# Banks next to each other, loads without held transfers, and a new order of issue in a fused attention and channel-mix kernel

## The chip, the cores and the metric

The kernel runs on one core of one Trainium2 chip. The metric is the device time of one execution in microseconds (us), less is better. Three runs of the kernel before gave 128.08, 128.44 and 128.81 us. A further execution was taken with the hardware profiler; all rows below are from that one.

The core has five engines, each with a queue of its own that is worked off strictly in order: PE (matrix products, results to PSUM only), DVE (vector), ACT (scalar), POOL (GpSimd, which does not touch PSUM here) and SP (here it only issues transfers). They meet through semaphores. PSUM has eight banks of 512 float32 for each of 128 partitions.

## The reference

Two layers in a row, for 4 batches, 4 heads, 1088 positions and head size 32:

```python
def phi(x):                                  # sketch of degree 2: r = 8, so 64 features
    a = einsum('rd,bhsd->bhsr', S1, x)
    b = einsum('rd,bhsd->bhsr', S2, x)
    return einsum('bhsi,bhsj->bhsij', a, b).reshape(..., 64)
q_p, k_p = phi(q), phi(k)
kv  = einsum('bhsf,bhsd->bhfd', k_p, v)      # 64 x 32 for each head
num = einsum('bhsf,bhfd->bhsd', q_p, kv)
den = einsum('bhsf,bhf->bhs', q_p, k_p.sum(axis=2)) + 1e-6
x   = (num / den) as [4, 1088, 128]

xk = mu_k * x + (1 - mu_k) * x_prev          # x_prev: one position earlier
xr = mu_r * x + (1 - mu_r) * x_prev
k  = relu(xk @ w_k)                          # 128 -> 1024
v  = (k * k) @ w_v                           # 1024 -> 128
out = sigmoid(xr @ w_r) * v
```

## The kernel before, in words

Everything is one long list of small tasks, the string `ORDER` (L26). Each entry names a function, its indices, the engine that is to do it (`V` DVE, `A` ACT, `G` POOL, `P` DVE reading PSUM directly) and, after `@`, the PSUM banks that it writes. A loop at L583 calls the functions in that order. The order of the list is the order in which each engine gets its instructions; a tracker in the framework adds a semaphore wait wherever an instruction touches a tile that an instruction of another engine has written or still reads. All of PSUM is one tile, `PS`, of eight banks.

The first stage works batch by batch (0 to 3). For the keys: transposes `kt` on DVE, projection `kproj` on PE, copy `abev`, outer product `kp` (POOL or DVE), and `kvmm` on PE, then `kvev`, `kdmm`, `kdev` which lay `kv` out as weights in `kvw`. For the denominators: `zmm`, `zev`, `wmm`, `wsq`. For the queries: `qt`, `abw` on PE, copy `abwev`, then `pw`, `den`, `an` and the outer product `qp`. The result x is built by PE transposes `pt`, copies `ptev`, the product `xp` into a pair of banks, its copy `xpev`, and `tt`, `ttev`, `xt`, `xtev`, `xs` for the last 64 positions of each batch. Batch 3 takes another way: transposes `tr` on DVE and the product `xn` into four banks, copied by `xnev`.

The second stage works on 9 groups of columns: two groups of 512 for each batch, and group 8 of 256 with the last positions of all batches. `xk` and `xr` mix x with its shift (on POOL this is two instructions, L483 and L488; on DVE one, L491, L493 or L496). `f1.g.c` (L523) makes one of four parts of the hidden layer: two products of 128x512 into a pair of banks. `relu.g.c` (L529) on ACT turns both banks of the pair into a bf16 tile `k1` (six buffers). `sq.g.c` squares it into `k2` (eight buffers), on DVE at L264 or on ACT at L538. `f2.g.c` (L550) multiplies with `wv`, eight products of 128x128, and accumulates over c in one bank for each group. `rr` (L559) and `sig` (L565) make the gate, `fin` (L568) multiplies on DVE, `st` (L578) stores.

The pair of banks is a view of `PS` with a stride: `f1.2.1@24` writes banks 2 and 4 through `PS[:, 2:5:2]`, and `relu.2.1` reads both in one instruction:

```python
    def pair(banks, n):
        i, j = banks
        return PS[:, i:j + 1:j - i, :n]
```

Before the first stage, `zz` (L191) multiplies zeros into a bank that nobody reads. The loads are issued by SP in the order of `LOADS` (L24). An entry with a `+` is a transfer of four bytes out of a tile that is being loaded into `held` (L159): SP can issue it, and so all that stands behind it, only when that load has landed.

## Time and profile before

| | |
|---|---|
| median of three runs (lowest, highest) | 128.44 us (128.08, 128.81) |
| the profiled execution | 127.39 us |
| its span, first to last instruction | 125.6 us |
| mean granted PE clock in the span | 0.903 |
| busy PE, DVE, ACT, POOL | 88.4, 76.1, 61.5, 50.0 us |
| first product of the second stage (`f1.0.1`) starts | 29.83 us |
| last `relu` starts | 120.43 us |

The profiled execution's 127.39 us is 1.8 us more than its span: what lies ahead of the first and behind the last instruction. In the page's groups the columns are: line, engine, operation, tiles out and in, shape, count; busy us and mean ns of one; idle time of the engine just before them, and what ended most of it. In the timeline the columns are start, length, engine, line, operation, count, and in brackets the idle time before it and who ended it. In the list of waits they are total us, number of times, and the longest.

### The profile page before, as it was taken

To read this page: it belongs to the slowest core of one execution; us is meant where nothing else is said; L and a number is where in the kernel's file an instruction comes from. 1 tells how busy PE (TensorE), PEld (TensorE's weight loads), DVE (VectorE), ACT (ScalarE), POOL (GpSimd) and SP (SyncE) were. 2 spreads that over 40 slices of the span, in tenths; PEclk is the share of its full clock that TensorE was granted. 3 is DMA by queue.
4 is the path that set the end of the run, shared out by engine and by line. 5 is a ranking of instruction groups with operands and counts; after the bars stand their busy time and mean duration, and the time that the engine had idled before them with its cause. 6 is when DMAs were issued, how large, how long until landed. Compare 5 with 4: busy or idle time off the path is not lost.

```text
span 125.6 us, 3716 instructions
## 1 busy us (share of the span) xinstructions
PE 88.4 (70%) x1592; PEld 64.0 (51%) x1603; DVE 76.1 (61%) x133; ACT 61.5 (49%) x91; POOL 50.0 (40%) x60
## 2 busy tenths in 40 slices
PE   6998999985658699665489345999675682558240
PEld 2577997863346487433358124576453461428220
DVE  3694298637476965929508971869859870624301
ACT  2210225861986498663138037356859346264140
POOL 5258089499900259407005910145997000000000
PEclk9999999999999999999658975559999999779985
DMA  3994991928290000030002000000003150400331
GB/s 110 315 277 131 333 246 31 348 81 249 73 304 16 5 0 8 17 72 0 0 5 59 25 0 0 5 0 3 5 6 77 27 141 5 82 2 0 84 84 44
DMA packets 9998, 10.26 MB, mean 82 GB/s; under 512 B 1020, under 2 KB 7422, under 8 KB 9982
## 3 DMA queue, kind: packets, MB, share of 16 engines
q1 hardware_dynamic: 9370, 9.77, 27.0%
q10 hardware_dynamic: 612, 0.27, 0.9%
q8 instruction: 12, 0.20, 0.7%
q14 instruction: 4, 0.03, 0.1%
HBM read 7.80 MB, written 2.23 MB: 80 GB/s over the span
## 4 chain that ended last, share of the span: by engine, by line
PE 51%; DVE 21%; ACT 17%; issue 7%; ACTq 2%; another core or an unknown queue 0%; DVEq 0%
ACT k L529 15%; PE ps L550 14%; PE ps L364 8%; PE ps L523 8%; DVE k L264 7%; PE ps L282 6%; DVE q L568 4%; PE ps L191 3%; PE ps L330 3%; PE ps L450 3%; DVE XT L491 2%; PE ps L441 2%; DVE kv L261 1%; ACTq L578 1%; DVE xk L493 1%
## 5 line engine op out<-in xcount | busy, mean ns | idle before, releaser
L529 ACT ACTIVATE k<-ps 128x1024 bf16<-128x1024 f32 (+1 forms) x36 | 34.4, 976 | 35.8 <-PE ps L523 13.2
L550 PE MATMUL ps<-wv,k 128*128 128x128 bf16 x272 | 23.9, 240 | 17.3 <-ACT k L529 17.2
L550 PEld LDWEIGHTS <-k 128*128 128x128 bf16 x272 | 20.5, 109 | 28.0 <-issue 25.4
L523 PE MATMUL ps<-xk,wk 128*128 128x512 bf16 x54 | 19.8, 437 | 8.1 <-ACT k L529 3.0
L264 DVE TENSOR_TENSOR k<-k 128x1024 bf16<-128x1024 bf16 (+1 forms) x28 | 21.5, 815 | 5.6 <-ACT k L529 5.6
L264 POOL TENSOR_TENSOR qp<-an,abw 128x512 f32<-128x512 f32 (+3 forms) x10 | 18.4, 1855 | 8.2 <-DVE an L264 7.9
L568 DVE TENSOR_TENSOR q<-ps,q 128x512 f32<-128x512 f32 (+1 forms) x9 | 5.9, 660 | 16.2 <-PE ps L550 9.9
L264 POOL TENSOR_TENSOR kp<-ab 128x1024 f32<-128x1024 f32 (+1 forms) x5 | 10.6, 2132 | 4.6 <-ACT ab L257 2.4
L364 PE MATMUL ps<-SQ,qT 128*32 128x96 f32 (+5 forms) x288 | 11.1, 265 | 1.3 <-ACT k L529 1.0
L364 PEld LDWEIGHTS ps<-SQ,qT 128*32 128x32 f32 (+1 forms) x288 | 9.5, 137 | 2.7 <-ACT k L529 1.3
L523 PEld LDWEIGHTS <-wk 128*128 128x128 bf16 x72 | 6.4, 107 | 8.1 <-issue 6.4
L282 PE MATMUL ps<-SK,kT 128*32 128x64 f32 (+1 forms) x234 | 8.5, 259 | 0.3
L538 ACT ACTIVATE k<-k 128x1024 bf16<-128x1024 bf16 (+1 forms) x8 | 8.0, 1000 | 0.0
L441 PE MATMUL ps<-ident,qp 128*128 128x128 f32 x48 | 7.8, 302 | 0.0
L282 PEld LDWEIGHTS ps<-SK,kT 128*32 128x32 f32 (+1 forms) x234 | 7.2, 140 | 1.1 <-issue 1.0
L441 PEld LDWEIGHTS ps<-ident,qp 128*128 128x128 f32 x48 | 6.5, 160 | 1.9 <-POOL kp L264 0.9
L257 ACT COPY ab<-ps 128x256 f32<-128x256 f32 (+1 forms) x6 | 2.4, 398 | 9.1 <-PE ps L282 9.1
L267 DVE STREAM_TRANSPOSE kT<-kv 128x576 f32<-128x576 f32 x8 | 5.9, 752 | 1.2 <-DMA kv<-in_k_dram 1.2
L330 PE MATMUL ps<-kp,kv 128*32 128x64 f32 x288 | 5.9, 222 | 0.4 <-issue 0.4
L261 DVE COPY X<-ps 128x512 f32<-128x512 f32 (+1 forms) x4 | 2.3, 570 | 6.3 <-ACT k L529 3.7
L493 DVE SCALAR_TENSOR_TENSOR xk<-ps,rat,X 128x512 bf16<-128x512 f32 x5 | 3.7, 749 | 3.7 <-ACT ab L257 2.7
L565 ACT ACTIVATE q<-ps 128x512 f32<-128x512 f32 (+1 forms) x9 | 5.1, 573 | 1.6 <-PE ps L559 1.6
(99 smaller groups left out, 119.9 us busy)
## 6 DMA issues: line engine op xcount, KB each, us to landing
q<-in_q_dram SPq DMA_DIRECT2D x4, 544.0 KB
out_dram<-q SPq DMA_DIRECT2D x28, 64.0 KB, 1.8
kv<-in_k_dram SPq DMA_DIRECT2D x3, 544.0 KB
kv<-in_v_dram SPq DMA_DIRECT2D x8, 144.0 KB, 2.7
kv<-in_v_dram SPq DMA_DIRECT2D x8, 128.0 KB, 5.6
kv<-in_k_dram SPq DMA_DIRECT2D x2, 272.0 KB, 3.0
wk_f<-in_moe_w_k_dram SPq DMA_DIRECT2D x1, 512.0 KB
wv_f<-in_moe_w_v_dram SPq DMA_DIRECT2D x1, 512.0 KB
```

The source lines that it names most:

```text
L264: (nc.gpsimd if eng == "G" else nc.vector).tensor_mul(o, x, y)
L267: nc.vector.transpose(_ap(kT[b % 2][:, 0, 2 * y], [[32, 2], [128, 9], [1, 32]]), kin[b][:, y].rearrange("p (c m d) -> p c m d", c=2, m=9))
L282: nc.tensor.matmul(_ap(o[i:i + w, 32 * (m - m0):32 * (m - m0) + 32], [[n, 2], [1, 32]]), kT[b % 2][:, m].rearrange("p c a -> p (c a)")[:, ...
L330: nc.tensor.matmul(o[32 * h:32 * h + 32, :F], vin[b][:, h, m, :], sb["kp", b, j][:, 4 * (m - KG[j][0]) + h].rearrange("p i j -> p (i j)"), ...
L364: nc.tensor.matmul(_ap(o[c:c + m], [[w * step, H], [1, w]], w * i0), qT[b % 2][:, 4 * t:4 * t + 4, :].rearrange("p u a -> p (u a)")[:, c:c ...
L441: nc.tensor.transpose(o[:, P * h:P * h + P], x.rearrange("p y i j -> p (y i j)"), ident[:])
L523: nc.tensor.matmul(h[:, c, :], wk[:, 2 * cp + c].rearrange("p y f -> p (y f)"), x, skip_group_check=True)
L529: nc.scalar.activation(o[:, :, :size(g)], h, RELU)
L538: nc.scalar.activation(o[:, :, :n], k1[:, :, :n], mybir.ActivationFunctionType.Square)
L550: nc.tensor.matmul(o[:, i * P:i * P + P], k2[:, c, i * P:i * P + P], wv[:, 2 * cp + c, :], start=(cp == 0 and c == 0 and i == 0), stop=(cp ...
L565: nc.scalar.activation(osb(g), ps["r", g][:, :size(g)], SIGMOID)
L568: nc.vector.tensor_mul(osb(g), ps["o", g][:, :size(g)], osb(g))
```

## The change

The functions stay as they are. `LOADS` loses its five `+` entries, and v0 now comes ahead of k1, w0 right after q1. `ORDER` is a new list of the same 397 tasks. In it

- every pair of banks is two neighbours (`@01`, `@23`, `@34`, `@56`, `@67`, `@12`); before there were pairs such as `@24`, `@36`, `@57`, `@16`, `@02`;
- the fours of `xn` are both `@1234` (before `@0123` and `@1234`);
- there are 13 products with zeros at the start (`zz.8`, `zz.2`, `zz.2`, `zz.1`; before 6, 1, 2, 1), and `smm` stands behind eight of them in place of six;
- most tasks stand elsewhere, and some 50 have another engine: among them `qp.2` (both parts) goes from POOL to DVE, five more `xk` go to POOL, `ptev` goes from 7 on ACT and 5 on DVE to 10 and 2.

The functions that the lists call are unchanged. The diff, cut (first and some later lines of each list):

```diff
-LOADS = "k0 q0 k1 v0 +k1 q1 w0 +v0 v1 w1 w2 +v1 k2 q2 +q2 v2 k3 +v2 q3 v3"
+LOADS = "k0 q0 v0 k1 q1 w0 v1 w1 w2 k2 q2 v2 k3 q3 v3"
 
 ORDER = """
-zz.6@7 smm@0 kt.0.0 zmu@1 sset sqset kt.0.1 zz.1@2 mumm@0 muset kproj.0.0.T@2 abev.0.0.V qt.0.0 zset qt.0.1
-kproj.0.1.W@3 abev.0.1.A zz.2@0 zmm.0@3 zev.0.A zz.1@2 wmm.0 kp.0.0.G kp.0.1.G abw.0.1.q.W@1 kt.1.0 abw.0.0.q.T@2
...
-ptev.0.0.1.A den.1.0.36 an.0.20.36.G kt.2.1 qp.0.20.28.G qp.0.28.36.G pt.0.1.0@0 ptev.0.1.0.A pt.0.1.1@1 ptev.0.1.1.A
-wrset.G xt.0 xtev.0.A kt.2.0 xs.0.A xp.0.0@24 xpev.0.0.A kvmm.1.0@5 xp.0.1@01 xpev.0.1.A kvmm.1.1 kproj.2.0.T@3
-abev.2.0.A xk.0.0.P f1.0.1@24 kproj.2.1.T@6 wvset.0.G xk.0.1.P xr.0.1.P abev.2.1.V f1.1.0@37 relu.0.1.A relu.1.0.A
...
-f2.1.3 f1.2.0@57 abwev.3.0.f.A sq.0.3.V kdmm.2 relu.2.0.A kdev.2.A abw.3.1.f.T@6 fin.1 st.1.S f1.2.1@24 relu.2.1.A
-f2.0.0@3 an.2.0.36.G qp.2.0.20.G kp.3.0.P xp.1.1@57 kvmm.3.0@0 abwev.3.1.f.V sq.2.0.A xpev.1.1.V xk.1.1.P f1.2.2@24
-xr.1.2.G xk.1.2.V pw.3.0.36.V xr.1.1.P f2.0.1 relu.2.2.A f1.2.3@16 f2.0.2 relu.2.3.A f1.3.0@24 f2.0.3 relu.3.0.A
...
-sq.8.2.V f2.7.3 fin.7 st.7.SA xr.2.2.G relu.8.3.A f2.8.1 rr.8@3 f2.8.2 sq.8.3.A f2.8.3 sig.8 fin.8 st.8.S
+kt.0.0 zz.8@7 smm@0 zz.2@2 mumm@1 zmu@2 sset sqset kt.0.1 kproj.0.0.T@0 abev.0.0.A zset muset qt.0.0 kproj.0.1.W@2
+abev.0.1.A zz.2@0 zmm.0@2 zev.0.A kp.0.0.G zz.1@1 wmm.0 qt.0.1 wsq.0 abw.0.0.q.T@1 abwev.0.0.q.V kp.0.1.G
+abw.0.0.w.W@2 pw.0.0.20.P den.0.0.20 an.0.0.20.G abw.0.1.q.W@1 abwev.0.1.q.A kvmm.0.0@2 kvmm.0.1 kvev.0.A qp.0.0.8.G
+qp.0.8.20.G kt.1.0 abw.0.1.w.T@1 kt.1.1 kproj.1.0.T@0 kproj.1.1.W@3 abev.1.0.A abev.1.1.A kdmm.0 kdev.0.A qt.1.1
+pw.0.20.36.P den.0.20.36 pt.0.0.0@1 zmm.1@3 zev.1.A qt.1.0 wkset.1.A pt.0.0.1@2 ptev.0.0.1.A ptev.0.0.0.A wkset.0.V
+wmm.1 wsq.1 tt.0@4 abw.1.0.f.W@3 an.0.20.36.G qp.0.20.28.G ttev.0.A kp.1.1.G abwev.1.0.f.A kp.1.0.P abw.1.1.f.W@2
+abwev.1.1.f.A wvset.0.A xp.0.0@01 qp.0.28.36.G xpev.0.0.A pw.1.0.36.G kt.2.1 xt.0 xtev.0.A wvset.1.A pt.0.1.0@3
+kvmm.1.0@2 wrset.G ptev.0.1.0.A pt.0.1.1@5 ptev.0.1.1.A kt.2.0 kproj.2.0.T@4 xs.0.G den.1.0.36 xk.0.0.P abev.2.0.A
+kp.2.0.P kvmm.1.1 f1.0.1@01 kvev.1.A kdmm.1 an.1.0.36.G qp.1.0.20.G kdev.1.A kproj.2.1.T@5 xp.0.1@67 relu.0.1.A
+f1.0.3@23 qt.2.0 kt.3.0 xpev.0.1.A relu.0.3.A kvmm.2.0@4 f1.0.0@67 abev.2.1.A pt.1.0.1@0 kt.3.1 kproj.3.1.T@2 tt.1@3
...
+relu.2.3.A f2.0.0@7 sq.0.2.A kvmm.3.0@2 xp.1.1@01 abwev.2.1.f.V sig.0 xr.0.2.V wsq.3 f2.0.1 xpev.1.1.V f1.2.0@56
+f2.0.2 sq.1.1.A relu.2.0.A pw.2.0.36.G xk.1.1.G f1.2.1@34 relu.2.1.A xr.1.1.P den.2.0.36 f2.0.3 abw.3.0.f.T@0
...
+sig.7 f2.6.1 f1.8.1@67 sig.6 f2.7.3 f1.8.2@34 relu.8.1.A fin.7 st.7.SA sq.8.1.V f2.6.2 f1.8.3@12 relu.8.2.A sq.8.2.V
+f2.8.0@6 f2.6.3 relu.8.3.A sq.8.3.A f2.8.1 fin.6 st.6.SA rr.8@3 sig.8 f2.8.2 f2.8.3 fin.8 st.8.S
```

## The prediction

> **What bounds the kernel now.** I read the page first (busy shares, costliest groups), then the list of waits, then the timeline where the longest waits are, and last the busy time by stretch.

> ```profile
> PE 88.4 (70%) x1592; PEld 64.0 (51%) x1603; DVE 76.1 (61%) x133; ACT 61.5 (49%) x91; POOL 50.0 (40%) x60
> ...
> L529 ACT ACTIVATE k<-ps 128x1024 bf16<-128x1024 f32 (+1 forms) x36 | 34.4, 976 | 35.8 <-PE ps L523 13.2
> ```

> No engine is full; the line that costs most idle time is `relu` (L529), whose engine stood still for 35.8 us just before its 36 instructions. The list of waits says for whom:

> ```profile
> PE ps L550 <- ACT k L529: 17.2, 14, 2.4
> ...
> ACT k L529 <- PE ps L550: 9.3, 8, 3.1
> ...
> ACT k L529 <- DVE q L568: 5.3, 3, 2.6
> ...
> DVE q L568 <- ACT k L529: 4.7, 1, 4.7
> ```

> Three of these pairs should not exist. `f2` (L550) reads squares, not `relu`'s output; `relu` reads what `f1` wrote, not `f2`; `fin` (L568) and `relu` share nothing. Two places in the timeline show why they wait all the same.

> ```profile
> 49.41 1.05 ACT L538 ACTIVATE k<-k 128x1024 bf16<-128x1024 bf16 x1
> ...
> 54.16 1.02 ACT L529 ACTIVATE k<-ps 128x1024 bf16<-128x1024 f32 x1 [1.34 <-PE ps L523]
> ...
> 55.23 0.61 PE L550 MATMUL ps<-wv,k 128*128 128x128 bf16 x8 [1.11 <-ACT k L529]
> ...
> 60.77 0.59 PE L523 MATMUL ps<-xk,wk 128*128 128x512 bf16 x1 [2.45 <-DVE xr L493]
> 61.15 1.06 PE L550 MATMUL ps<-wv,k 128*128 128x128 bf16 x8
> 62.25 1.02 ACT L529 ACTIVATE k<-ps 128x1024 bf16<-128x1024 f32 x1 [3.08 <-PE ps L550]
> ```

> The first three rows are `sq.0.0`, `relu.2.1` and `f2.0.0@3`. The square was done at 50.46, yet `f2` started at 55.23, just after `relu.2.1` (54.16 + 1.02), which reads banks 2 and 4. Bank 3 lies between. The last three are the second product of `f1.2.3@16` (bank 6), `f2.0.2` (bank 3) and `relu.2.3` (banks 1 and 6). The product waited 2.45 us for `xr.1.1`, which reads banks 5 and 7; `relu.2.3` had its own two products at 61.36 and started when `f2.0.2` ended, at 62.2. Bank 6 lies between 5 and 7, bank 3 between 1 and 6. I conclude that the tracker takes a strided pair for everything from its first to its last bank. So PE waits for ACT, ACT then waits for PE, and the two take turns.

> **The change part by part.**

> *Neighbouring pairs.* A span of two neighbours holds no third bank, so these waits have no cause left. Directly in question are 17.2 on PE, 9.3 + 5.3 on ACT and 4.7 on DVE; they overlap, so they cannot be summed. What is late next is work: `f2` then waits for its square, `f1` for `relu` to free its two banks. I therefore cost the second stage by its fullest engine.

> ```profile
> 29.83:120.43 90.60, 60.97 (x1038) 42.86 (x1048) 57.79 (x89) 50.00 (x66) 31.20 (x25) 0.89 0.16 40
> 45.00:50.00 5.00, 4.73 (x178) 4.08 (x180) 2.47 (x7) 4.55 (x10) 4.56 (x5) 1.00 0.02 5
> ```

> Columns: stretch, length, busy PE, PEld, DVE, ACT, POOL, granted clock. From the first `f1` to the last `relu` 90.6 us pass with DVE busy 57.8 and ACT 50.0 (64% and 55%). The fullest five microseconds show what in-order queues can reach: 95% on PE, 91% on ACT.

> *Engines that change.* Prices:

> ```profile
> L257 ACT COPY kv<-ps 128x512 f32<-128x512 f32 x7 | 3.8, 600 | 0.4 <-PE ps L441 0.4
> L261 DVE COPY kv<-ps 128x512 f32<-128x512 f32 x5 | 3.3, 665 | 0.0
> L491 DVE SCALAR_TENSOR_TENSOR XT<-X,rat 128x64 bf16<-128x64 f32 x4 | 3.6, 898 | 0.0
> L264 DVE TENSOR_TENSOR kp<-ps,ab 128x1280 f32<-128x1280 f32 x2 | 3.0, 1479 | 0.0
> L264 DVE TENSOR_TENSOR k<-k 128x1024 bf16<-128x1024 bf16 x25 | 20.5, 862 | 4.0 <-ACT k L529 4.0
> ```

> DVE gives up three `ptev` (2.0) and the four small `xk` (3.6), and takes `qp.2` (at the price of `kp` on DVE 1.48 for 1280 and, in proportion, 1.18 for 1024) and one square more (0.86): 2.1 less. ACT gains three `ptev` (1.8) and loses one square; the rest are copies of under 0.6, some in each direction. POOL loses `qp.2` and gets five more mixes, which I take as even. So the work stays: I take 56 us on DVE and 50 on ACT for the second stage. The unknown is how full DVE can be kept: 95% would make 59 us, the 64% of before 87.5. I take 88% (64 us), nearer to the fullest stretch, since the stretches of before are emptied by the waits that go. ACT is then at 78%.

> *Front.* The first `f1` waits for `xk.0.0`, and that in the new list stands behind POOL, whose work ahead of it is `kp.0.0`, `kp.0.1`, `an`, `qp.0` in four pieces, `an`, `kp.1.1`, `pw.1`, `wrset`, `xs.0`.

> ```profile
> 7.75 4.31 POOL L264 TENSOR_TENSOR kp<-ab 128x1280 f32<-128x1280 f32 x2 [2.19 <-DVE ab L261]
> ...
> 16.11 0.46 POOL L264 TENSOR_TENSOR an<-abw,den 128x160 f32<-128x160 f32 x1 [4.05 <-ACT ab L257]
> 16.65 2.54 POOL L264 TENSOR_TENSOR qp<-an,abw 128x512 f32<-128x512 f32 x2
> 19.16 0.41 POOL L264 TENSOR_TENSOR an<-abw,den 128x128 f32<-128x128 f32 x1
> 19.64 2.10 POOL L264 TENSOR_TENSOR qp<-an,abw 128x512 f32<-128x512 f32 x2
> 21.72 1.23 POOL L244 TENSOR_SCALAR wr<-wr_f,omu 128x128 bf16<-128x128 f32 x1
> ...
> 29.02 1.41 DVE L493 SCALAR_TENSOR_TENSOR xk<-ps,rat,X 128x512 bf16<-128x512 f32 x2 [2.66 <-ACT ab L257]
> 29.83 0.38 PE L523 MATMUL ps<-xk,wk 128*128 128x512 bf16 x1 [1.36 <-DVE xk L493]
> ```
> ```profile
> L264 POOL TENSOR_TENSOR kp<-ab 128x1024 f32<-128x1024 f32 x3 | 5.9, 1953 | 2.4 <-ACT ab L257 2.4
> L264 POOL TENSOR_TENSOR pw<-abw 128x288 f32<-128x288 f32 x1 | 0.8, 800 | 7.5 <-DVE abw L261 7.5
> L259 POOL COPY X<-X 128x31 f32<-128x31 f32 x1 | 0.7, 656 | 3.0 <-ACT X L257 3.0
> ```

> 4.31 + 0.46 + 2.54 + 0.41 + 2.10 + 1.95 + 0.80 + 1.23 + 0.66 = 14.5 us. If POOL starts at 7.75 as before and waits 2 us on the way (before, `an` alone waited 4.05), `xs.0` ends at 24.3, `xk.0.0` (half of 1.41) at 25.0, and `f1` starts at about 25.1, 4.7 earlier than 29.83.

> *Zero products.* Whether POOL waits 2 us or 5 hangs on PE's clock at the start.

> ```profile
> 1.18 2.74 PE ps L191 x6
> ...
> 38.53 0.55 PE ps L523 x2
> ```
> ```profile
> 14.54 1.06 PE L282 MATMUL ps<-SK,kT 128*32 128x64 f32 x32
> ...
> 44.11 0.65 PE L282 MATMUL ps<-SK,kT 128*32 128x64 f32 x32
> ```

> Six zero products take 2.74 us, 0.46 each, where two products of that shape later take 0.55, 0.28 each; and 32 projections take 1.06 at 14.54 and 0.65 at 44.11. So PE ran at half speed until at least 14.5, by durations (the page's clock line shows full speed there, and is no witness for the start). Two more zero products ahead of `smm` cost 2 x 0.46 = 0.9 us: `smm` starts at 4.9, `kproj` and all behind it about 1 later, if the speed stays as it was. If the fuller start releases the clock early, the `abw` products and projections between 6 and 16 shrink by about a third and the front gains some 4 us. I bound the first `f1` by 25.1 and 29.8 (no gain) and take 25.5. [...]

> *Loads.* Five held transfers go. Behind them stand only loads, so nothing else is released. k1 now lands after v0, about 0.55 MB later, but its transpose stands later too. Price between 0 and the 1.2 us below, more traffic meeting the first load; I take 0, since the first four transfers are the same.

> ```profile
> DVE kT L267 <- DMA kv<-in_k_dram: 1.2, 1, 1.2
> ```

> *End.* Last `relu` to the last instruction:

> ```profile
> 119.47 0.86 ACTq L578 DMA_DIRECT2D out_dram<-q  x2
> 120.43 0.60 ACT L529 ACTIVATE k<-ps 128x512 bf16<-128x512 f32 x1 [2.60 <-DVE q L568]
> ```

> 125.6 - 120.43 = 5.2; the new list puts the issue of `st.6` (0.86) on ACT ahead of `sig.8`, so 6.

> Sum: 25.5 + 0.6 (first `f1` to its `relu`) + 64 + 6 = 96 us of span, + 1.8 around it = 98, and the median stands 1.05 above the profiled execution (128.44 to 127.39): 99 us.

> **The rivals.**

> *Given back by DVE and POOL.* DVE's squares stretch when POOL works beside them:

> ```profile
> 67.25 5.86 DVE L264 TENSOR_TENSOR k<-k 128x1024 bf16<-128x1024 bf16 x3
> 67.48 5.08 POOL L264 TENSOR_TENSOR qp<-an,abw 128x1280 f32<-128x1280 f32 x2 [7.87 <-DVE an L264]
> ```

> Three squares took 5.86 us where 25 average 0.86. A dozen large two-input POOL instructions stand behind the first `f1` in the new list; at some 1.9 us each they hold DVE for up to 23. For it: DVE is the fullest engine. Against it: 56 us contain such stalls already. Half of it makes 111, all of it 122.

> *The waits are only renamed.* If `f2`'s squares, not the banks, were what ended late, the turn-taking stays and only the front moves: 124 to 129. Against it: the square of the quoted `f2` was done 4.8 us early.

> *Slower: PE stays at half clock.* With the banks of a pair freed only in list order, PE could be idle often enough that its clock is taken away through the second stage.

> ```profile
> 60.00:65.00 5.00, 3.12 (x20) 2.12 (x20) 1.49 (x4) 1.02 (x1) 0.00 (x0) 0.54 0.01 3
> ```

> There the clock was 0.54 after PE had waited 2.45 for `xr`, and eight `f2` products took 1.06 instead of 0.61. 34 such groups at +0.45 are 15 us; 36 pairs of `f1` at 2 x 0.46 (the slow zero products) instead of 0.55 are 13; with the front's gain of 4.3 lost too, 99 + 15 + 13 + 4 = 131. It decides if the clock is below about 0.55 nearly throughout. Against it: such stretches were followed by full clock once PE was fed, and PE has less to wait for. [...]

> **How the numbers follow.** Forecast (waits go, 91 to 106) 0.66; given back (106 to 124) 0.24; renamed 0.03; half clock 0.07. The low end is 91: DVE at 95% (5 us less), POOL's 2 us of waiting in the front gone, and the issue of `st.6` hidden (0.9). The high end, 115, takes in half of the second case. A measurement here tells 0.5% (0.6 us) from nothing. Faster 0.91, same 0.02, slower 0.07.

> **What would show it.** Right: no row of L550 waiting on L529 worth over 3 us in all; ACT's idle before `relu` under 15; DVE the fullest engine from `f1` on; first `f1` near 25; at most a few windows under full clock. Wrong: `f2` waiting as long for DVE's squares (second rival), long squares beside POOL (first), a granted clock near 0.55 (third), a first `f1` at 29 or later (front).

## The result and the profile after

| | before | after |
|---|---|---|
| median of four runs (lowest, highest), us | 128.26 (126.44, 128.81) | 94.58 (93.61, 96.37) |
| the profiled execution, its span, us | 127.39, 125.6 | 93.61, 91.8 |
| first `f1` starts, us | 29.83 | 30.32 |
| first `f1` to last `relu`, us | 90.6 | 55.82 |
| last `relu` to the end, us | 5.2 | 5.7 |
| mean granted PE clock | 0.903 | 0.985 |

After takes 0.736 of the time of before, 95% interval 0.7155 to 0.7565. (Some executions of a kernel take over 1.5% longer than its fastest; ratios with an interval leave these out, medians take in all.) All of the gain lies between the first `f1` and the last `relu`; the front has gained nothing. The page after, its busy shares, the chain that ended last by engine, and two of its groups:

```profile
PE 82.0 (89%) x1562; PEld 60.8 (66%) x1576; DVE 70.3 (77%) x124; ACT 62.1 (68%) x97; POOL 48.5 (53%) x67
...
PE 71%; DVE 17%; issue 4%; ACT 2%; ACTq 2%; DVEq 0%
...
L529 ACT ACTIVATE k<-ps 128x1024 bf16<-128x1024 f32 (+1 forms) x36 | 33.8, 980 | 4.5 <-PE ps L523 1.7
...
L550 PE MATMUL ps<-wv,k 128*128 128x128 bf16 x272 | 20.5, 219 | 1.0 <-ACT k L538 0.3
```

ACT stood still for 4.5 us before its 36 `relu` (before 35.8), and `f2` no longer waits for `relu` at all. In the list of waits after, what is left of the turn-taking:

```profile
ACT k L529 <- PE ps L523: 1.7, 2, 1.5
...
ACT k L529 <- PE ps L550: 1.4, 2, 1.2
```

The busy time by stretch from the first `f1` to the last `relu` (stretch, length, busy PE, PEld, DVE, ACT, POOL, granted clock, busy share of the DMA engines, GB/s):

```profile
30.32:86.14 55.82, 52.22 (x1060) 37.80 (x1069) 53.52 (x83) 49.83 (x70) 30.91 (x31) 1.00 0.14 33
```

DVE is busy for 96% of it (before 64%), PE for 94%, ACT for 89%. The chain of work that ended last shows which of them decides where; these are neighbouring pieces late in the stage (start, length, what):

```profile
69.54 0.43 PE ps L523 x2
69.97 0.45 PE ps L550 x8
70.41 0.43 PE ps L523 x2
70.85 0.45 PE ps L550 x8
71.30 0.62 PE ps L523 x2
71.97 0.68 DVE k L264
72.65 1.02 DVE xk L496
73.67 1.69 DVE xr L496
```

First PE goes from product to product with nothing between, then DVE decides for 3.4 us. From 75.4 to 84.0 the chain is PE's again; earlier in the stage it runs through DVE from 39.7 to 44.6 and, with short gaps, from 57.9 to 65.3.

The front after, in the timeline:

```profile
6.90 3.19 PE L282 MATMUL ps<-SK,kT 128*32 128x64 f32 x48
...
8.77 4.31 POOL L264 TENSOR_TENSOR kp<-ab 128x1280 f32<-128x1280 f32 x2 [2.46 <-ACT ab L257]
...
12.25 5.33 PE L364 MATMUL ps<-SQ,qT 128*32 128x64 f32 x58
...
17.02 0.47 POOL L264 TENSOR_TENSOR an<-abw,den 128x160 f32<-128x160 f32 x1 [3.93 <-DVE den L394]
...
21.29 0.41 POOL L264 TENSOR_TENSOR an<-abw,den 128x128 f32<-128x128 f32 x1 [1.19 <-DVE den L394]
...
27.03 0.80 POOL L264 TENSOR_TENSOR pw<-abw 128x288 f32<-128x288 f32 x1 [0.83 <-ACT abw L257]
...
28.68 0.65 DVE L493 SCALAR_TENSOR_TENSOR xk<-ps,rat,X 128x512 bf16<-128x512 f32 x1
...
29.51 0.87 PE L330 MATMUL ps<-kp,kv 128*32 128x64 f32 x32
...
30.32 0.39 PE L523 MATMUL ps<-xk,wk 128*128 128x512 bf16 x1
```

POOL starts 1.0 us later than before and waits 3.93 + 1.19 + 0.83 = 5.95 us on its way, mostly for the `abw` products (58 in 5.33 us) by way of `pw` and `den`. `xk.0.0` is done at 29.33 (28.68 + 0.65), and `f1` then stands 1.0 us behind two tasks on PE.

### The profile page after: what moved, and what is told of

The parts are those of the page before. It is cut to its first block, busy times and chain, and to the rows that moved or that the text cites. A ratio compares the mean times of both kernels' runs of the same rounds, so it can differ in the third digit from the quotient of the medians.

```text
span 91.8 us, 3656 instructions
## 1 busy us (share of the span) xinstructions
PE 82.0 (89%) x1562; PEld 60.8 (66%) x1576; DVE 70.3 (77%) x124; ACT 62.1 (68%) x97; POOL 48.5 (53%) x67
## 4 chain that ended last, share of the span: by engine, by line
PE 71%; DVE 17%; issue 4%; ACT 2%; ACTq 2%; DVEq 0%
PE ps L550 11%; PE ps L523 11%; PE ps L364 11%; PE ps L282 8%; PE ps L330 7%; PE ps L191 6%; PE ps L441 6%; DVE k L264 3%; DVE kv L412 3%; DVE xr L496 3%; PE ps L450 3%; PE ps L559 2%; DVE q L568 2%; DVE X L261 2%; DVE xk L493 2%
## 5 line engine op out<-in xcount | busy, mean ns | idle before, releaser
L529 ACT ACTIVATE k<-ps 128x1024 bf16<-128x1024 f32 (+1 forms) x36 | 33.8, 980 | 4.5 <-PE ps L523 1.7
L264 DVE TENSOR_TENSOR k<-k 128x1024 bf16<-128x1024 bf16 (+1 forms) x29 | 20.6, 754 | 1.2 <-ACT k L529 1.2
L550 PEld LDWEIGHTS <-k 128*128 128x128 bf16 x272 | 16.9, 98 | 6.9 <-issue 2.0
L550 PE MATMUL ps<-wv,k 128*128 128x128 bf16 x272 | 20.5, 219 | 1.0 <-ACT k L538 0.3
L523 PE MATMUL ps<-xk,wk 128*128 128x512 bf16 x51 | 16.2, 381 | 0.6 <-DVE xk L493 0.6
L264 POOL TENSOR_TENSOR qp<-an,abw 128x512 f32<-128x512 f32 (+3 forms) x8 | 13.8, 1732 | 0.2
L264 POOL TENSOR_TENSOR kp<-ab 128x1024 f32<-128x1024 f32 (+1 forms) x5 | 10.6, 2133 | 2.6 <-ACT ab L257 2.5
L364 PEld LDWEIGHTS ps<-SQ,qT 128*32 128x32 f32 (+1 forms) x252 | 10.7, 147 | 1.4 <-issue 0.9
L282 PE MATMUL ps<-SK,kT 128*32 128x64 f32 (+1 forms) x240 | 8.3, 260 | 0.0
L264 POOL TENSOR_TENSOR an<-abw,den 128x288 f32<-128x288 f32 (+2 forms) x4 | 2.5, 626 | 10.6 <-DVE den L394 5.6
L257 ACT COPY ab<-ps 128x320 f32<-128x320 f32 (+1 forms) x6 | 2.4, 400 | 7.8 <-PE ps L282 7.8
L282 PEld LDWEIGHTS ps<-SK,kT 128*32 128x32 f32 (+1 forms) x240 | 7.1, 140 | 0.9 <-issue 0.3
L441 PE MATMUL ps<-ident,qp 128*128 128x128 f32 x48 | 7.2, 280 | 0.1
L523 PEld LDWEIGHTS <-wk 128*128 128x128 bf16 x72 | 5.5, 99 | 2.5 <-issue 1.3
L568 DVE TENSOR_TENSOR q<-ps,q 128x512 f32<-128x512 f32 (+1 forms) x9 | 5.8, 649 | 1.5 <-ACT q L565 1.5
L191 PE MATMUL ps<-zero 128*128 128x512 bf16 x12 | 5.9, 627 | 1.2 <-DVE warm L142 1.2
L538 ACT ACTIVATE k<-k 128x1024 bf16<-128x1024 bf16 (+1 forms) x7 | 6.9, 995 | 0.0
L257 ACT COPY abw<-ps 128x480 f32<-128x480 f32 (+2 forms) x5 | 2.5, 490 | 6.5 <-PE ps L364 6.5
L267 DVE STREAM_TRANSPOSE kT<-kv 128x576 f32<-128x576 f32 x8 | 5.7, 746 | 1.1 <-DMA kv<-in_k_dram 1.1
L330 PEld LDWEIGHTS ps<-kp,kv 128*32 128x32 f32 x288 | 5.3, 125 | 1.8 <-issue 1.0
```

The costliest lines, as they stand in the source:

```text
L191: nc.tensor.matmul(PS[:, banks[0], :w], zero[:, :P], zero[:, :w], skip_group_check=True)
L264: (nc.gpsimd if eng == "G" else nc.vector).tensor_mul(o, x, y)
L267: nc.vector.transpose(_ap(kT[b % 2][:, 0, 2 * y], [[32, 2], [128, 9], [1, 32]]), kin[b][:, y].rearrange("p (c m d) -> p c m d", c=2, m=9))
L282: nc.tensor.matmul(_ap(o[i:i + w, 32 * (m - m0):32 * (m - m0) + 32], [[n, 2], [1, 32]]), kT[b % 2][:, m].rearrange("p c a -> p (c a)")[:, ...
L330: nc.tensor.matmul(o[32 * h:32 * h + 32, :F], vin[b][:, h, m, :], sb["kp", b, j][:, 4 * (m - KG[j][0]) + h].rearrange("p i j -> p (i j)"), ...
L364: nc.tensor.matmul(_ap(o[c:c + m], [[w * step, H], [1, w]], w * i0), qT[b % 2][:, 4 * t:4 * t + 4, :].rearrange("p u a -> p (u a)")[:, c:c ...
```

## The experiments

Each run gives a median over its executions beside runs of the kernel before on the same chip. Ratios are to before; an interval stands where one was given. Where a run is set against after, the two medians come from different jobs; the median of before itself lay between 126.8 and 128.3 us in them, so that a difference of under some 1.5 us from after is not told from nothing.

### Is it the spans of the strided pairs?

**After, with its banks renamed.** The list stays; only the number of each bank changes, so that `@23` becomes banks 3 and 5, `@56` 2 and 4, `@67` 4 and 6. Five of six pairs are strided again.

```diff
-            args.append([int(i) for i in banks])
+            args.append([(0, 1, 3, 5, 7, 2, 4, 6)[int(i)] for i in banks])
```

> The changed kernel with its banks renamed, nothing else: banks 0 to 7 become 0, 1, 3, 5, 7, 2, 4, 6, so that five of the six pairs have a stranger between them again (23 is 35, 12 is 13, 34 is 57, 56 is 24, 67 is 46) and xn writes 1, 3, 5, 7. Same instructions, same order, same loads. Spans theory (the tracker takes a strided pair for all from its first to its last bank): waits of f2 (L550) on relu (L529) come back, several us in all, ACT's idle time before relu rises from 4.5 to over 12, and the time goes to 103 to 118 us. Order theory (the new list and its engines carry the gain, the banks do not matter): 94 to 96 us, no row of L550 waiting on L529.

Measured: 107.91 us (106.50 to 112.33), ratio 0.8463 (0.8358 to 0.8569), 13 us above the changed kernel. Waits and stretch of this kernel:

```profile
DVE k L264 <- ACT k L529: 5.7, 4, 3.3
DVE q L568 <- PE ps L550: 5.6, 3, 2.7
...
PE ps L523 <- ACT k L529: 4.3, 8, 0.9
...
PE ps L559 <- ACT k L529: 2.8, 3, 2.0
PE ps L550 <- ACT k L529: 2.8, 4, 1.5
```
```profile
29.28:99.08 69.80, 55.03 (x1060) 38.50 (x1069) 51.48 (x83) 50.53 (x70) 27.74 (x31) 1.00 0.12 27
```

```profile
L529 ACT ACTIVATE k<-ps 128x1024 bf16<-128x1024 f32 (+1 forms) x36 | 34.2, 978 | 11.8 <-PE ps L523 4.0
```

The same work on the same engines in the same order takes 69.8 us instead of 55.8, at full clock. The turn-taking is back, spread over more pairs than in before: `f2` behind `relu`, of which after has no row, is only 2.8 us of it, and ACT's idle time before `relu` is 11.8 us, where after has 4.5 (just under the 12 expected).

**Before, with every pair read in two instructions,** one for each bank (`relu`, `xpev`, and `xk` and `xr` where they read PSUM). Its strided pairs and its list stay.

The part for `relu`; `xpev`, `xk` and `xr` are split in the same way:

```diff
-            nc.scalar.activation(o[:, :, :size(g)], h, RELU)
+            for c in range(2):
+                nc.scalar.activation(o[:, c, :size(g)], h[:, c], RELU)
```

> The kernel before, its list and banks unchanged, but each instruction that reads a pair of banks (relu, xpev, xk and xr from PSUM) is made as two, one for each bank, so that no access spans a third bank. Cost by the rows: a relu of 512 takes 0.60, two 1.20, against 1.02, so 32 times 0.17, 5.6 us more on ACT, and some 3 on DVE. Spans theory: the 17.2 us of L550 on L529 and the 9.3 back go, and in spite of the dearer relu the time falls to 103 to 116 us. Order theory: no wait worth naming goes, the dearer relu shows, 128 to 134 us.

Measured: 103.77 us (103.03 to 104.98), ratio 0.8193 (0.8116 to 0.8271): 23 us less than before, though there are 39 more instructions on ACT. In its groups (its `relu` is L533, `f1` L526):

```profile
L533 ACT ACTIVATE k<-ps 128x512 bf16<-128x512 f32 (+1 forms) x72 | 36.1, 607 | 7.7 <-PE ps L526 4.2 <-DVE q L572 2.0 <-PE ps L554 1.3
```

The idle time before `relu` falls from 35.8 to 7.7 us with nothing moved: `relu` waits 1.3 us for `f2` (before 9.3) and 2.0 for `fin` (before 5.3), and no wait of `f2` for `relu` is left.

**After, split in the same way,** as a control for what splitting costs or brings by itself.

> The changed kernel with the same splitting as in the second experiment: every instruction that reads a pair of banks is made as two, one for each bank. If the gain of the second experiment came only from spans that no longer hold a foreign bank, the splitting has nothing to remove here and only its price is left: there relu's work rose from 34.4 to 36.1 us and DVE's busy time from 76.1 to 80.1, so 95 to 99 us against 94.6 for the changed kernel. If a finer grain by itself brings something (a bank comes free half a relu, 0.5 us, earlier, 36 times), it would be faster than the changed kernel, 88 to 93 us, and then the second experiment would have overstated what the spans cost.

Measured: 95.06 us (94.19 to 96.77), against 94.58. Where no pair is strided, splitting brings nothing. So the gain of the run before is not one of finer grain: a strided pair is waited for as a span, and reading it bank by bank ends nearly all of that. The three runs agree; this is shown.

The spans are not the whole gain, though. From the first `f1` to the last `relu`, before takes 90.6 us, before with split reads 67.5, after with strided pairs 69.8, and after 55.8. So the rest of the change (order, engines, loads) brings much of it too: 11.7 us where no pair is waited for as a span, 20.8 where most are. The renamed pairs hold one foreign bank each, those of before up to four (`@16`), which may be why the spans cost 14.0 us there and 23.1 in before. No run separates the order from the engines.

### What sets the front?

**After with fewer zero products** (6, 1, 2, 1 as in before; 8, 2, 2, 1 in after). Start of the line:

```diff
-kt.0.0 zz.8@7 smm@0 zz.2@2
+kt.0.0 zz.6@7 smm@0 zz.1@2
```

> The changed kernel with 10 zero products as before (6, 1, 2, 1) in place of 13 (8, 2, 2, 1). Clock theory (the extra products release PE's clock earlier): PE stays slow longer and the first f1 comes later, 95.5 to 98 us. Rival (in the changed kernel the clock came at 21 us all the same, so the three products only delay smm): the start shifts by 3 times 0.43, 1.3 us earlier, 93 to 94.5 us, and the first f1 starts near 29.

Measured: 93.78 us (92.67 to 95.78), ratio 0.7387 (0.7302 to 0.7471): no difference. But its profile tells more than its time:

```profile
4.97 2.01 PE L282 MATMUL ps<-SK,kT 128*32 128x64 f32 x48
...
25.23 0.65 DVE L493 SCALAR_TENSOR_TENSOR xk<-ps,rat,X 128x512 bf16<-128x512 f32 x1
...
29.72 0.54 PE L330 MATMUL ps<-kp,kv 128*32 128x64 f32 x22 [3.27 <-issue]
30.19 0.39 PE L523 MATMUL ps<-xk,wk 128*128 128x512 bf16 x1
```

Here the clock was granted at 4.1 us, and the first 48 projections took 2.01 us, not 3.19. `xk.0.0` came 3.45 us earlier than in after. Yet the first `f1` starts at 30.19, since PE stood still for 3.27 us in the middle of a `kvmm`, 10 products into it, waiting for nothing that the profile shows.

Such a stop stands in all six profiles in which the clock came early and no load was held. From the traces' records, the number of weight loads that PE had done (the few waits that are recorded among them counted in), how long the next one was then missing and until when, and when the last 16 KB piece on the instruction queue ahead of that had landed:

```
fewer zero products   488 weight loads   3.43 us, to 29.72   piece landed 28.37
renamed banks         229                2.35 us, to 15.76                14.44
split after           229                2.39 us, to 15.57                14.17
                      488                2.94 us, to 30.82                29.12
narrow products       227                2.68 us, to 13.85                12.45
                      357                3.78 us, to 20.07                18.82
unheld, old order     229                3.16 us, to 16.71                15.26
four squares less     229                2.63 us, to 15.66                14.17
                      358                1.52 us, to 22.66                21.15
                      488                1.81 us, to 28.58                27.17
```

The stops stand at fixed counts, 227 to 229, 357 to 358 and 488, about 130 apart, whatever tasks the list has there: three zero products less moved the last one from 7 to 10 weights into its task. Each ends 1.2 to 1.7 us after a piece of program has landed. The kernel before with the loads of after has a shorter one, 1.09 us at 359. In all eleven profiles with the new list the weight load behind each of these counts starts at least 1.2 us after the landing of its piece (the first, second and third on that queue), though the loads just ahead of it may run up to 2.7 us before that landing. After itself comes to the three counts at 19.24, 25.52 and 29.80 us, 1.40, 1.40 and 1.46 after the landings, with pauses of at most 0.17 us (229, 358 and 488 are 221, 348 and 473 weight loads there, the rest waits). I conclude that PE had run out of its own program; that is inferred from these times, no trace names the cause. The stops, 1.5 to 3.8 us long in the table, come while the loads keep the DMA engines busy: with fewer zero products these were busy for 90% or more from 4.6 to 27.5 us and for 70% up to 29.8, and its stop lasts from 26.3 to 29.72.

**After with its six wide products made narrow** (the three shown, and `kproj.1.1`, `abw.1.0.f`, `abw.1.1.f`; only the tasks that change).

```diff
-kproj.0.1.W@2
+kproj.0.1.T@2
...
-abw.0.0.w.W@2
+abw.0.0.w.T@2
...
-abw.0.1.q.W@1
+abw.0.1.q.T@1
```

> The changed kernel with the six wide products (W: 18 weights of 128 columns) made in the narrow form (T). Before the clock is released 18 wide ones took 3.92 us and lay on the way to the first kvmm; 40 narrow weights took 1.06 us. If PE's work in the front sets the first f1, that comes 2 to 4 us earlier (26 to 28 instead of 30.3) and the time is 91 to 93 us. If the loads set the pace (in the changed kernel the last ones land at about 30.6 us and all DMA engines are busy until then), the front's products are early but the second stage starts its own way at the same time: within 1 us of the changed kernel, 93.6 to 95.5.

Measured: 95.75 us (95.30 to 97.08), 1.2 above after's median and not told from it. Neither expectation was met: the first `f1` came at 32.7, not earlier. The narrow forms are 156 more weight loads, so the same counts come earlier in its list, and the two stops of the table add up to 6.5 us. In this profile the granted clock was also down to 0.5 from 15.0 to 28.6 us; what each of the two cost is not separated.

**After with the loads of before,** its five held transfers included.

```diff
-LOADS = "k0 q0 v0 k1 q1 w0 v1 w1 w2 k2 q2 v2 k3 q3 v3"
+LOADS = "k0 q0 k1 v0 +k1 q1 w0 +v0 v1 w1 w2 +v1 k2 q2 +q2 v2 k3 +v2 q3 v3"
```

> The changed kernel with the loads of before: five held transfers, k1 ahead of v0. Theory of the prediction (the loads are hidden): within 0.5% of the changed kernel. Rival (loads that are held back arrive late for the tighter list): k2, q2 issued near 20 us and v2, k3 near 27 as before, so kt.2 and kt.3 wait on DVE, 1 to 5 us longer, 95.5 to 100 us.

Measured: 98.07 us (96.41 to 99.83), ratio 0.7676 (0.7570 to 0.7782), 3.5 us above after. No stop at the counts of the table, but data late:

```profile
DVE kT L267 <- DMA kv<-in_k_dram: 9.8, 3, 4.6
```

**After with the order of before's loads and no holding.**

```diff
+LOADS = "k0 q0 k1 v0 q1 w0 v1 w1 w2 k2 q2 v2 k3 q3 v3"
```

> The changed kernel with the loads in the order of before (k1 ahead of v0, w0 as before) but with no held transfers. With the loads of before whole, the changed kernel took 98.1 us. If the holding is what cost those 4 us, this one takes 93.6 to 95.5; if the order cost them (v0 after k1 makes the first kvmm late), 97 to 99.

Measured: 95.17 us (93.44 to 97.07), as after. So the 3.5 us are the holding, not the order of the loads.

**Before with the loads of after.**

> The kernel before with the changed kernel's list of loads (no held transfers, v0 ahead of k1, w0 after q1). If the loads are worth their 4 us to any list, 122 to 125 us against 127 to 128. If they are worth it only where the second stage can take up what comes earlier, the bank waits swallow it: 126 to 129 us, with the last load landing near 31 us in place of 39.

Measured: 131.09 us (130.34 to 132.88) against 126.82: slower by 4.3, which neither side expected. Its second stage took 90.67 us, as in before (90.60); the first `f1` came at 33.86 instead of 29.83. PE's clock was granted at 23.9 us there, in before at 16.0. Whether the loads cause the late clock, this one profile cannot tell; it stays open.

### Is DVE the bound of the second stage?

**After without four squares of DVE,** those of group 6; `relu` writes straight into the tiles that `f2` reads there, so the result is another. The part in `sq`:

```diff
         k1 = sb["k1", g, cp]
+        if g == 6:
+            sb["k2", g, cp] = k1
+            return
```

> The changed kernel without the four squares of group 6: its relu writes straight into the tiles that the second product reads, so that group's part of the result is made without squaring. All four stand on DVE late in the second stage (seven squares took 4.02 us there, 0.57 each, so 2.3 us of work goes). If DVE, 96% full from the first f1 to the last relu, sets that stage alone, it gets 2 to 2.5 us shorter: 53.3 to 53.8 us instead of 55.8, and the time 92 to 92.7. If PE (52.2 of 55.8 us busy) and ACT (49.9) stand just behind it, less than 1 us comes of it: 93.7 to 94.6.

Measured: 95.18 us (92.29 to 96.36), against 94.58. The profiled execution, the shortest of the four, took 92.29, 1.3 less than that of after; 1.2 of this lie ahead of the first `f1` (29.09). The stretch:

```profile
29.09:84.82 55.73, 53.19 (x1073) 37.78 (x1069) 49.74 (x78) 49.74 (x71) 29.21 (x31) 1.00 0.15 33
```

DVE has 3.8 us less to do and the stretch is as long as in after; PE is busy for 95% of it. DVE is the fullest engine of after, but does not set the stage alone. The squares left out stand between 80 and 84 us in after, where the chain is PE's; what less work on DVE would bring where the chain runs through DVE (39.7 to 44.6, 57.9 to 65.3, 72.0 to 75.4) is not tested.

### A version with a shorter front

**After with lightly held loads.** A load goes out when the one two or three before it has landed; k2 goes ahead of w1.

```diff
+LOADS = "k0 q0 v0 k1 +q0 q1 +v0 w0 +k1 v1 +q1 k2 w1 w2 +v1 q2 +k2 v2 +q2 k3 +v2 q3 v3"
```

> The changed kernel with loads held lightly: a load is sent out when the one two or three before it has landed, so that fewer transfers are in flight at a time, and k2 goes out ahead of w1. Theory: the front of the changed kernel is paced by the fetch of PE's own program (pieces of 16 KB), which comes late while many loads are in flight: in the runs with an early clock PE stopped for 2.2 to 3.6 us at the same count of PE instructions (227 to 229, 357, 488), whatever the list. With fewer transfers in flight these stops go, and k2 is there at about 18 to 20 us (with before's loads DVE waited 4.6 us for it): first f1 at 24 to 27 us, 89 to 92.5 us in all. Rival: the loads' sum (7.8 MB, the last one landing at 30.6 us) is the pace, whatever is in flight: first f1 at 28.5 to 31, 93.5 to 96 us. If the holds make the loads late, as those of before did, 96 to 98.

Measured: 93.06 us (91.79 to 93.44), no stop at 229, 357 or 488. Timeline and stretch:

```profile
22.66 0.75 DVE L493 SCALAR_TENSOR_TENSOR xk<-ps,rat,X 128x512 bf16<-128x512 f32 x1 [0.65 <-POOL X L259]
...
23.55 0.60 PE L523 MATMUL ps<-xk,wk 128*128 128x512 bf16 x2
...
30.22 1.44 DVE L267 STREAM_TRANSPOSE kT<-kv 128x576 f32<-128x576 f32 x2 [3.87 <-DMA kv<-in_k_dram]
```
```profile
23.55:85.26 61.71, 55.53 (x1075) 38.67 (x1069) 53.73 (x83) 50.54 (x72) 31.40 (x31) 0.97 0.25 62
```

The first `f1` comes 6.8 us earlier than in after, and 5.9 of that is lost again in the second stage, where k3 is late. The clock came early here (4.6 us) and late in after, but the five profiles with an early clock, the wide products of after and no load held have their first `f1` at 29.1 to 31.3, so some 5.5 us or more of it are the loads. The time missed the 89 to 92.5 us expected.

**The same with only q3 and v3 held behind v1.**

```diff
+LOADS = "k0 q0 v0 k1 +q0 q1 +v0 w0 +k1 v1 +q1 k2 w1 w2 +v1 q2 v2 k3 +q2 q3 v3"
```

> The lightly held loads of the run before, with the last three waits but one taken out: q2, v2 and k3 go out as soon as v1 has landed, only q3 and v3 wait for q2. There the first f1 came at 23.55 us, but the second stage took 61.7 us instead of 55.8, with DVE waiting 3.9 us for k3 and 1.9 for q3 and PE 2.3 for the projection behind them. If that lateness is all that ate the gain, k3 lands at about 26 and the stage takes 56 to 58 us from a first f1 at 23.5 to 24.5: 86.5 to 90 us. If more in flight makes PE's program late again, a stop of over 1 us stands at 229, 357, 488 or one 130 further on, and it is 90 to 93.

**The same with nothing held behind v1** (without `+q2`).

> As the run before it, but with no wait behind v1 at all (q2, v2, k3, q3, v3 go out together). If PE's program is late only while many loads are in flight, the stop comes back at the count of 488 or the next one (about 620), 1 to 3 us, and it stands 1 to 3 us behind the run before it: 88 to 92 us. If the early waits were what counted, both are the same within 1 us.

Measured: 92.07 us (89.64 to 93.70) with q3 and v3 held, 92.90 (91.82 to 94.51), ratio 0.7272 (0.7213 to 0.7331), with nothing held. In the first, k3 is nearly in time (DVE waits 1.1 us at most for a k) and the stretch takes 57.7 us, but two stops are back, 0.96 us at 229 and 1.57 at 488. The second of them:

```profile
25.39 0.58 PE L330 MATMUL ps<-kp,kv 128*32 128x64 f32 x25 [1.40 <-issue]
25.91 0.60 PE L523 MATMUL ps<-xk,wk 128*128 128x512 bf16 x2
```

In the second, against what I expected, no stop came back at 488 or later; instead k3 was late again, with q3 and v3 sent out right behind it:

```profile
32.02 1.44 DVE L267 STREAM_TRANSPOSE kT<-kv 128x576 f32<-128x576 f32 x2 [4.73 <-DMA kv<-in_k_dram]
```

This profiled execution took 94.51 us, the longest of its six; whether k3 was as late in the shorter ones is not known.

That the stops come from many loads in flight is therefore borne out only in part: with nothing held and an early clock all six profiles have them, with loads held throughout (as in before, or lightly) neither profile does, but with loads let go behind v1 one has them and one has not. In after itself, whose clock came late, PE came to the three counts 1.40, 1.40 and 1.46 us after the landings, as long after them as the stops end elsewhere (1.2 to 1.7).

The version with q3 and v3 held is the fastest seen: 0.725 of before in its job, where after has 0.737 in its own. The two were not timed side by side, so the 2.5 us between their medians have no interval.

## Why the prediction was right, point by point

Forecast 99 us, range 91 to 115; it came to 94.6, in the main for the reason given, but with two terms wrong in opposite directions.

- **Spans, turn-taking gone:** shown. Four of the five signs named hold: no row of `f2` waiting on `relu`, 4.5 us of ACT's idle before `relu` (under 15), DVE the fullest engine from the first `f1` on, and no window under full clock between 20.9 and 89.1 us. The fifth, a first `f1` near 25, failed, and the sign of a wrong front (29 or later) came. The prediction put nearly the whole gain of the stage down to these waits; the renamed banks show that the new list brings much of it with spans still there.
- **Second stage, 64 us (with the 0.6 to the first `relu`, 64.6):** measured 55.8, so 8.8 too long. The mechanism was right and the size off. DVE had 53.5 us of work for the 56 assumed, and was kept at 96% where I took 88%. "The fullest engine" as the bound was too simple: the chain changes between DVE and PE's own products, and 3.8 us less on DVE where the chain is PE's changed nothing. Three engines (53.5, 52.2, 49.8 us) lie within 4 us of each other there.
- **Front, first `f1` at 25.5 (bounds 25.1 to 29.8):** this step failed; it came at 30.3, outside its bounds. Three parts of it: POOL started at 8.77, not 7.75; it waited 5.95 us on the way, where I put 2; and `f1` stood 1.0 us behind other work on PE. (POOL's own work took 0.8 less than I put, and `xk.0.0` stood 0.3 behind `den` on DVE.) I costed POOL's queue from its own durations and took PE ahead of it from before, while PE took 5.33 us for 58 `abw` products in the new list, before its clock was granted (5.26 in the chain that ended last, against 2.85 with renamed banks, where the clock came early). The bounds allowed for no loss at all, and should have. PE's program, of which the prediction has no term, may have paced the front as well: the first `f1` came 1.8 to 2.6 us after the third piece had landed (28.34 in after) in nine of the eleven profiles with the new list.
- **Zero products:** that a fuller start releases the clock sooner was my estimate, and no run shows it: with 10 of them the clock came at 4.1 us, with 13 at 20.9 in after, and the time was the same. The half of the sentence that an early clock would gain "some 4 us" is true up to `xk.0.0` (3.45 us) and not beyond: PE's stop took it back.
- **Loads, 0:** wrong in size, and not hidden. The new list loses 3.5 us if its loads are held as before, so letting them go was needed; the old list loses 4.3 us if they are let go.
- **End, 6 us:** 5.7.
- **From span to median:** 1.8 around the span and 1.05 to the median; measured 1.8 and 1.0.
- **Rival "given back by DVE and POOL":** its mechanism is there and small.

```profile
39.80 2.17 DVE L264 TENSOR_TENSOR k<-k 128x1024 bf16<-128x1024 bf16 x1
```
```profile
37.11 4.32 POOL L264 TENSOR_TENSOR kp<-ab 128x1024 f32<-128x1024 f32 x2
```

This square took 2.17 us beside POOL's `kp`, where the median is 0.68. All 29, each by itself, add up to 21.9 us; 26 at 0.68 and the 3 of half size at 0.41 would take 18.9, so the stretching of the squares costs some 3.0 us, not the 12 to 23 of that rival.
- **Rival "only renamed":** fell; the stage shrank by 35 us. **Rival "half clock":** fell; the granted clock was 1.00 from the first `f1` to the last `relu`, and PE's longest pause there was 1.3 us.

The sum came out right because the front's +4.8 and the second stage's -8.8 partly cancel; the profile before carried the cause, not these two sizes. That it came within 4.4 us is to that extent luck.

## What to carry to other kernels

Where a tracker adds the waits, ask what extent it gives to a strided view: waits between instructions that share no data are the sign, and cutting the view into contiguous pieces tests it in one run, with the price of the extra instructions in the same profile. Cost a queue that is to start earlier together with the engine that feeds it, at the clock that this engine has there. When a front of many small products is made faster, look next at where PE stops for no reason shown, and set the counts and times against the landings on the instruction queue.

## What the runs showed of the hardware that was not expected

```profile
0.00:5.00 5.00, 3.81 (x17) 1.29 (x18) 2.02 (x7) 1.49 (x2) 1.81 (x16) 1.00 0.57 166
5.00:10.00 5.00, 5.00 (x58) 3.93 (x56) 3.38 (x11) 0.43 (x1) 2.16 (x8) 1.00 1.04 292
```

(The clock column has 1.00 there because the records begin with the first grant; the first 48 projections' 3.19 us in after, for 2.01 with the early clock, show the slow one.) PE was busy almost throughout and yet got no full clock for some ten us more; what tells the two cases apart stays open.
- **An earlier clock changed little.** After (granted at 20.9) and the run with fewer zero products (4.1) have their first `f1` within 0.2 us of each other. Their third pieces of program landed at 28.34 and 28.37.
